# A block-diagonal product of 576 columns as two products of 288 columns in a two-bank PSUM tile

## The chip, the cores and the metric

One core of one Trainium2 chip runs the whole program. The metric is the device time of one execution in microseconds. Engine names in the profile: PE is TensorE, PEld its weight loads, DVE is VectorE, ACT is ScalarE, POOL is GpSimd, SP is SyncE.

## The reference, cut to what matters

```python
kv  = einsum('bhsd,bhse->bhde', k, v)          # 8 x 8 heads, 576 tokens, 64 wide
out = einsum('bhsd,bhde->bhse', q, kv)
x   = out / sqrt(mean(out * out) + 1e-6) * g_norm
h   = x.reshape(4608, 512) @ w_in              # 512 -> 2048
y   = (h * erf(softplus(h))) @ w_out           # 2048 -> 512
```

Nearly all the work is in the last two products. The attention part is small, and the kernel slips it between them, pair of heads by pair of heads.

## The kernel before

The tokens go in groups. A group of the large products has 512 tokens: the first 512 of each of the eight sequences, and a ninth group made of the 64 left over from each ("tail"). While PE works on one group, the attention of the next is computed for its four pairs of heads. From the third group on, the mean of squares is taken from a high and a low part in the faster fp32r format (on the chain of before 0.23 us for 512 columns, against 0.86 for the two records of an fp32 product, L520); the code calls that `halves`. (The prediction and the code count groups from 0, so the changed groups are 2 to 7; the expectations of the runs count from 1 and say 3 to 8.)

The kernel keeps eight PSUM buffers of [128, 512] fp32, here called banks. Six serve the large products. Two, the pool `ps_at`, serve the attention, with four one-bank tiles per pair that take turns:

```python
def bank(name):                                 # one bank: [128, 512] fp32
    pool, tag = (pools or {}).get(name, (ps_at, "at"))
    return pool.tile([P, G], FP32, name=name, tag=tag)

def products():
    kv_ps = st["kv"] = bank("kv_ps")
    ...                                         # PE: k.T v of two heads into kv_ps
    if p % 2 == 0:                              # PE: tail of q, transposed, for two pairs
        nc.tensor.transpose(kv_ps[:, q_tail], q_last[:, p // 2], ident)
    ...
    for i in range(2):                          # DVE: the two blocks to SBUF
        nc.vector.tensor_copy(out=bd[s, s], in_=kv_ps[s, s])
    if p % 2 == 0:
        tails[T] = attp.tile([P, P], FP32, name="qT_last", tag="t")
        nc.vector.tensor_copy(out=tails[T], in_=kv_ps[:, q_tail])
    st["tail"] = tails[T][:, p % 2 * R : p % 2 * R + R]
    qt_ps = bank("qt_ps")
    for j in range(J):                          # PE: q transposed
        nc.tensor.transpose(qt_ps[:, j * P : j * P + P], qs[:, j], ident)
    nc.scalar.copy(st["qT"], qt_ps)             # ACT

def apply():
    qT, o_ps, kv_ps = st["qT"], bank("se_ps"), st.pop("kv")
    nc.tensor.matmul(kv_ps[:, o_tail], lhsT=bd, rhs=st.pop("tail"), ...)   # 64 columns
    nc.tensor.matmul(o_ps, lhsT=bd, rhs=qT, ...)                           # 512 columns
    nc.vector.tensor_copy(out=x_last[...], in_=kv_ps[:, o_tail])
    nc.scalar.activation(qT, o_ps, AF.Square)
# then halve() [DVE], mean() [PE, ACT], norm() [DVE: u, u, x], split() [ACT, DVE]
```

The pieces stand at fixed places among the large products: `products` at the head of a batch, `apply` two products later, and so on. In the timelines of this case the engines work through their instructions in the order in which the code issues them: in before a kv is done at 658.3 us, but VectorE, with the last eviction (e) ahead of that copy, stands idle for 0.46 us until that can run at 660.98, and copies kv at 661.59.

## Time and profile before

| | before |
|---|---|
| time, median of the first three runs | 954.99 us (953.88 to 955.01) |
| span of the profiled run | 952.2 us |
| PE busy | 929.1 us, 98% |
| mean granted clock of PE | 0.998 |
| pair to pair in the steady part, kv to kv | 24.72 and 24.84 us in turn |

PE is the bound. The lines of the page, of the chain of waits and of PE's timeline that carry this are in the prediction below.

### The profile page before, as it was taken

Reading aid. Unit: us, or ns where it says so; the run is one execution under the profiler, and the core shown is the slowest. Engines: PE = TensorE matmul, PEld = TensorE weight load, DVE = VectorE, ACT = ScalarE, POOL = GpSimd, SP = SyncE. Lnnn points to the kernel's source line nnn. Section 1 sums busy time; section 2 is a strip of 40 time slices with the busy share of each in tenths; the row PEclk is TensorE's granted clock in tenths of the full one; section 3 lists DMA queues with packets and bytes.
Section 4 is the critical chain, followed back from the end, with each engine's and each line's share of the span. In section 5 each row is a group of like instructions: output and inputs, shape, how many; then the busy total and the mean of one; then the engine's idle time right before and its main releaser. Section 6 shows DMA issues by size and latency. Waiting matters only on the chain.

```text
span 952.2 us, 11746 instructions
## 1 busy us (share of the span) xinstructions
PE 929.1 (98%) x4272; PEld 684.7 (72%) x4272; DVE 740.4 (78%) x1054; ACT 616.1 (65%) x825; POOL 2.4 (0%) x10
## 2 busy tenths in 40 slices
PE   6999999999998999999999999999999999999998
PEld 4444445665686788888888888888888788878886
DVE  3979958888575888888888888887887877777667
ACT  3889876777665666666666666666666666665552
POOL 1000000000000000000000000000000000000000
PEclk9999999999999999999999999999999999999999
DMA  9856505899699888898899988988896779768872
GB/s 256 276 163 212 167 9 218 307 347 337 212 356 339 275 286 282 289 315 301 290 304 309 303 293 314 322 290 283 290 337 251 264 256 348 283 248 304 338 272 65
DMA packets 111842, 259.78 MB, mean 273 GB/s; under 512 B 43864, under 2 KB 69544, under 8 KB 111784
## 3 DMA queue, kind: packets, MB, share of 16 engines
q1 hardware_dynamic: 110152, 256.73, 78.1%
q10 hardware_dynamic: 1568, 2.29, 0.8%
q8 instruction: 34, 0.56, 0.2%
q14 instruction: 24, 0.20, 0.1%
q0 software_dynamic: 64, 0.00, 0.0%
HBM read 224.40 MB, written 34.60 MB: 272 GB/s over the span
## 4 chain that ended last, share of the span: by engine, by line
PE 83%; ACT 6%; DVE 6%; DMA 3%; SPq 1%; issue 1%; DVEq 0%; ACTq 0%
PE n_ps L462 42%; PE m_ps L462 21%; PE o_ps L520 8%; PE h_ps L691 3%; PE se_ps L325 3%; PE kv_ps L297 2%; PE qt_ps L319 2%; DMA out_dram<-e 1%; DMA w_in_parts<-w_in 1%; SPq L136 1%; ACT w_e L215 1%; ACT L103 1%; DVE h L445 1%; ACT w_m L219 1%; DMA q_sb<-in_q_dram 1%
## 5 line engine op out<-in xcount | busy, mean ns | idle before, releaser
L462 PE MATMUL n_ps<-x_forms,w_in_parts 128*128 128x512 f32 x896 | 234.9, 404 | 5.0 <-ACT h L834 3.4
L462 PE MATMUL n_ps<-w_out_parts,g_forms 128*128 128x512 f32 x928 | 231.3, 391 | 0.0
L462 PEld LDWEIGHTS n_ps<-x_forms,w_in_parts 128*128 128x128 f32 x896 | 167.6, 189 | 49.4 <-issue 9.3
L462 PEld LDWEIGHTS n_ps<-w_out_parts,g_forms 128*128 128x128 f32 x928 | 174.2, 188 | 38.4 <-issue 1.7
L836 ACT ACTIVATE s<-h 128x512 f32<-128x512 f32 x112 | 71.1, 635 | 180.5 <-DVE h L445 180.5
L445 DVE TENSOR_TENSOR h<-m_ps,h 128x512 f32<-128x512 f32 x116 | 79.8, 688 | 68.3 <-ACT h L834 48.9
L462 PE MATMUL m_ps<-w_out_parts,g_forms 128*128 128x512 f32 x464 | 124.2, 389 | 0.0
L462 PE MATMUL m_ps<-x_forms,w_in_parts 128*128 128x512 f32 x448 | 120.0, 390 | 0.0
L520 PE MATMUL o_ps<-w_out_sb,h_sb 128*128 128x512 f32 x224 | 100.8, 593 | 0.3 <-DVE h_sb L642 0.3
L462 PEld LDWEIGHTS m_ps<-w_out_parts,g_forms 128*128 128x128 f32 x464 | 87.1, 188 | 18.1
L462 PEld LDWEIGHTS m_ps<-x_forms,w_in_parts 128*128 128x128 f32 x448 | 84.3, 188 | 17.8
L445 DVE TENSOR_TENSOR e<-m_ps,e 128x512 f32<-128x512 f32 x116 | 80.2, 692 | 17.9 <-PE m_ps L462 10.5
L440 DVE SCALAR_TENSOR_TENSOR e<-n_ps,e 128x512 f32<-128x512 f32 x88 | 60.3, 685 | 37.6 <-PE n_ps L462 37.5
L520 PEld LDWEIGHTS o_ps<-w_out_sb,h_sb 128*128 128x128 f32 x224 | 42.3, 190 | 48.9 <-issue 46.6
L834 ACT ACTIVATE h<-n_ps 128x512 f32<-128x512 f32 x112 | 65.6, 586 | 13.4 <-DMA out_dram<-e 9.5
L411 DVE SCALAR_TENSOR_TENSOR g_forms<-g_forms 128x1024 fp32r<-128x1024 f32 x58 | 71.1, 1225 | 2.0
L408 DVE TENSOR_TENSOR g_forms<-h,g_forms 128x1024 fp32r<-128x1024 f32 x58 | 70.6, 1217 | 1.8 <-ACT g_forms L405 1.4
L405 ACT ACTIVATE g_forms<-h 128x1024 fp32r<-128x1024 f32 x58 | 58.9, 1060 | 12.4 <-PE m_ps L462 9.8
L854 DVE TENSOR_TENSOR h<-h,s 128x1024 f32<-128x1024 f32 x56 | 65.9, 1218 | 0.7 <-ACT s L840 0.7
L691 PE MATMUL h_ps<-xT,w_in_sb 128*128 128x512 f32 x144 | 64.9, 594 | 0.8 <-DVE w_in_sb L240 0.6
L106 ACT ACT_TABLE_LOAD x44 | 56.5, 1283 | 0.7
L840 ACT ACTIVATE s<-s 128x1024 f32<-128x1024 f32 x56 | 56.2, 1052 | 0.3
(98 smaller groups left out, 1014.9 us busy)
## 6 DMA issues: line engine op xcount, KB each, us to landing
w_out_parts<-w_out SPq DMA_DIRECT2D x116, 768.0 KB
w_in_parts<-w_in SPq DMA_DIRECT2D x112, 768.0 KB
w_in<-w_new SPq DMA_DIRECT2D x16, 768.0 KB
q_sb<-in_q_dram SPq DMA_DIRECT2D x32, 256.0 KB
w_raw<-in_moe_w_out_dram SPq DMA_DIRECT2D x8, 1024.0 KB
out_dram<-e SPq DMA_DIRECT2D x32, 256.0 KB
k_sb<-in_k_dram SPq DMA_DIRECT2D x28, 287.5 KB
v_sb<-in_v_dram SPq DMA_DIRECT2D x28, 287.5 KB
```

Of the source, the lines that this page charges most:

```text
L106: nc.scalar.preload_act_table_set("softplus")
L405: nc.scalar.activation(high, x, AF.Copy, scale=1.0 + 2.0**-13)
L408: nc.vector.tensor_tensor(out=low, in0=x, in1=high.bitcast(FP32), op=ALU.subtract)
L411: nc.vector.scalar_tensor_tensor(out=both, in0=low.bitcast(FP32), scalar=SHIFT, in1=high.bitcast(FP32), op0=ALU.mult, op1=ALU.add,)
L440: nc.vector.scalar_tensor_tensor(out=out_, in0=ps, scalar=scale, in1=out_, op0=ALU.mult, op1=ALU.add)
L445: nc.vector.tensor_tensor(out=out_, in0=ps, in1=out_, op=ALU.add)
L462: nc.tensor.matmul(ps, lhsT=weights(form, k), rhs=moving(form, k), start=(form == forms[0] and k == 0), stop=(form == forms[-1] and k == 3),)
L520: nc.tensor.matmul(o_ps[j], lhsT=g[:, j * P : j * P + P], rhs=w_out_sb[:, f, :], start=(f == 0), stop=last,)
L691: nc.tensor.matmul(plain[i], lhsT=w_in_sb[:, c, i % FC * P : i % FC * P + P], rhs=xT[T][:, c, :], start=(c == 0), stop=(c == KC - 1),)
L834: nc.scalar.activation(h[:, i], n_ps, AF.Copy, scale=SHIFT - 1.0)
L836: nc.scalar.activation(s[:, i], h[:, i], AF.Softplus)
L854: nc.vector.tensor_tensor(out=part(h, half), in0=part(h, half), in1=part(s, half), op=ALU.mult)
```

## The change

The intent: two products of 288 columns carry the same 576 tokens in less time. In before the two products take 1.08 us, where 576 columns at the 0.858 us of 512 (two records of 0.429) would take 0.97. My estimate put the 0.11 us between these two numbers down to weight loads that the 64-column product is too short to cover. For this the tile has two banks, with 256 columns of the product and 32 of the tail in each, and the means go beside them in the other 256 columns. The diff, cut to its core:

```diff
         def bank(name):
+            if T >= FIRST:
+                return two_banks()[:, name in ("qt_ps", "se_ps")]
+        def two_banks():
+            if "two" not in st:
+                st["two"] = ps_two.tile([P, 2, G], FP32, name="at_ps", tag="at")
+            return st["two"]
 ...
-            if p % 2 == 0:
-                tails[T] = attp.tile([P, P], FP32, name="qT_last", tag="t")
-                nc.vector.tensor_copy(out=tails[T], in_=kv_ps[:, q_tail])
+            if halves:
+                tail = tails.pop(T) if p % 2 else kv_ps[:, P : P + R]
+                nc.vector.tensor_copy(out=st["qT"][:, :, HG:], in_=twofold(tail))
+                if p % 2 == 0:
+                    tails[T] = attp.tile([P, R], FP32, name="qT_next", tag="t")
+                    nc.vector.tensor_copy(out=tails[T], in_=kv_ps[:, P + R : 2 * P])
 ...
         def apply():
+            if halves:
+                for i in range(2):
+                    nc.tensor.matmul(two[:, i, : HG + HR], lhsT=bd, rhs=qT[:, i], ...)
+                nc.vector.tensor_copy(out=..., in_=two[:, :, HG : HG + HR])
+                nc.scalar.activation(qT, two[:, :, :HG], AF.Square)
 ...
         def mean(table=True):
+                for i in range(2):
+                    nc.tensor.matmul(ms[:, i], lhsT=mean_w, rhs=hi[:, i], start=True, stop=False)
+                    nc.tensor.matmul(ms[:, i], lhsT=mean_w, rhs=lo[:, i], start=False, stop=True)
 ...
+            at_room.close()
+            ps_two = ctx.enter_context(tc.tile_pool(name="ps_two", bufs=1, space=PSUM))
```

## The prediction

> **What bounds the kernel now.** I read the page first: the busy line, then the chain of work that ended last.
>
> ```profile
> PE 929.1 (98%) x4272; PEld 684.7 (72%) x4272; DVE 740.4 (78%) x1054; ACT 616.1 (65%) x825; POOL 2.4 (0%) x10
> ...
> PE 83%; ACT 6%; DVE 6%; DMA 3%; SPq 1%; issue 1%; DVEq 0%; ACTq 0%
> PE n_ps L462 42%; PE m_ps L462 21%; PE o_ps L520 8%; PE h_ps L691 3%; PE se_ps L325 3%; PE kv_ps L297 2%; PE qt_ps L319 2%; DMA out_dram<-e 1%; DMA w_in_parts<-w_in 1%; SPq L136 1%; ACT w_e L215 1%; ACT L103 1%; DVE h L445 1%; ACT w_m L219 1%; DMA q_sb<-in_q_dram 1%
> ```
>
> TensorE (PE) is the bound; the rest matters only where it makes PE stand. A busy matmul engine need not be at its peak, so I read the chain of waits in order of time, over one pair of heads in the steady part (columns: start us, us on the chain, what):
>
> ```profile
> 607.97 0.73 PE kv_ps L297 x20
> 608.71 0.26 PE kv_ps L305
> 608.97 0.44 PE qt_ps L319 x4
> 609.40 1.85 PE n_ps L462 x8
> ...
> 614.89 0.17 PE kv_ps L324 x2
> 615.06 0.91 PE se_ps L325 x2
> 615.98 1.84 PE n_ps L462 x8
> ...
> 624.17 0.23 PE ms_ps L346
> 624.40 0.23 PE ms_ps L347
> 624.63 1.83 PE n_ps L462 x8
> ```
>
> The chain here is PE without a hole, so an instruction that PE saves is time saved, and one that it gains is time lost. The diff touches three of these lines: L324 (tail product, 64 columns), L325 (block-diagonal product, 512 columns) and L346/L347 (mean of squares, high and low parts). "x2" for one matmul of the code says that an fp32 matmul runs as two passes; the fp32r mean runs as one.
>
> From 255 us to the end PE does stand in places, which I found in the timeline of PE (bracket: idle time, what ended it):
>
> ```profile
> 293.86 3.68 PE L462 MATMUL n_ps<-x_forms,w_in_parts 128*128 128x512 f32 x8 [3.41 <-ACT h L834]
> ...
> 309.87 0.80 PE L297 MATMUL kv_ps<-v_sb,k_sb 116*64 116x64 f32 x20
> 310.60 0.33 PE L305 MATMUL kv_ps<-ident,q_last 128*128 128x128 f32 x1
> 311.39 0.66 PE L319 MATMUL qt_ps<-ident,q_sb 128*128 128x128 f32 x4 [0.45 <-DVE x L378]
> ```
>
> The first is an h tile that waits for the store of e (the page puts 9.5 us of ACT's idle time before L834 on that DMA). The second matters to the change: kv of the next pair starts while the previous pair is still being normalised, and only the transposes wait for x, the last reader of the previous pair's product.
>
> [...] four 128-column transposes take 0.44 us on the chain, 0.11 each, although each weight-load record is about 190 ns long. [...] The trace has 227 in fp32r (0.91 for four m_ps) and 429 per fp32 pass (o_ps: 3.43 us for eight), so an fp32 pass streams at about half that rate. [...]
>
> **The change part by part**, per pair; groups 2 to 7 have 6 x 4 = 24 pairs.
>
> (1) Product, before: 0.17 + 0.91 = 1.08 us. Two 512-column passes at 0.429 are 0.86; the tail's two passes therefore cost 0.22, that is 0.11 each. [...] After: two matmuls of 288 columns, four passes. 0.429 x 288/512 = 0.241, say 0.243; four give 0.97. [...] Gain 0.11 us. The columns are the same (576)[...].
>
> (2) Mean: two fp32r matmuls of 512 columns, 0.46 us, become four of 256. [...] Four give 0.48. Loss 0.02.
>
> (3) DVE: twelve 128x128 tail copies of 292 ns go (L315), -3.5 us; 24 PSUM copies of 128x64 at 216 ns (as L326) come, +5.2, and 12 SBUF ones. For those: 128x512 casts take 418 ns and 128x1024 shifts 689 (L338, L207), so 0.53 ns a column and 147 fixed: 181 ns, +2.2 us. Sum +3.9 us on an engine with 22% idle. They stand behind the bd_kv copies, at 612.1 in the pair above; the product starts at 614.7. The new copies end by 612.6: hidden.
>
> (4) Buffers. Kv and transposes used to take whichever of two one-bank buffers was free; now one two-bank tile is reused, so kv, too, must wait for x. In the steady part:
>
> ```profile
> 631.74 0.75 DVE L378 SCALAR_TENSOR_TENSOR x<-se_ps,gm_col,u 128x512 f32<-128x512 f32 x1
> ...
> 632.74 0.80 PE L297 MATMUL kv_ps<-v_sb,k_sb 116*64 116x64 f32 x20
> ```
>
> x ends at 632.49; a handover takes 0.04 to 0.05 us (311.34 to 311.39). Slack is 0.2 us: no stall, but little. In the second to fourth pairs after the store's stall (309.87, 335.38, 360.10) kv starts before x has ended: 1.47, 0.52 and 0.30 us before. At 309.87 kv and the tail transpose, 0.73 + 0.2, now run after 311.38 instead of in the shadow of x; PE stood for 0.45 to 0.8 there anyway, so the transposes come about 0.75 us later. That delay also lets DVE and ACT catch up, so the next two (0.52, 0.30) should cost nothing more. Loss 0.75 us, once.
>
> Sum: 24 x (0.11 - 0.02) = 2.2 us gained. The four pairs of group 2 (0.36) lie ahead of the stall at 293, which ends with a DMA, and are probably swallowed there. 20 x 0.09 = 1.8; less 0.75 leaves about 1.05 us: 954.99 - 1.05 = 953.9.
>
> **Rivals.** (a) *Kv's wait for x becomes a stall in every pair.* For: slack is only 0.2 us, and u, x and the three ACT steps before them now read and write two runs of 256. Against: DVE's cost on cut patterns shows no extra per run: L854 works on four runs of 256 in 1218 ns[...]. If the chain grew by 0.3 us, 20 pairs would lose 0.1 to 0.2 each: 956 to 957. (b) *Weight loads become visible.* If a 256-column fp32r matmul were held to the 190 ns of a load record, the mean would cost 0.76, +0.3 a pair, +5 us net: 959 to 960. The transposes at 0.11 speak against. (c) *The tail comes free*: removing it saves all 0.22 a pair, 5 us, 950. Against: its 64 columns still stream. (d) *ACT's Square waits for DVE's copy of the tail.* In the steady part DVE copies at 618.33 to 618.54 and Square starts at 618.98, already in that order; in group 2 Square would come up to 1 us later (copy 153.18, Square 152.36), with ACT idle 3.7 us after it. Worth under 0.5 us in all.
>
> **Range and chances.** The certain terms are tenths of a microsecond a pair; 2% of 955 is 19 us, or 0.8 us on each of 24 pairs. Nothing above makes that: even (b) is a quarter of it. Three runs of before spread by 1.1 us, and the stretch held by DMA may move by a microsecond or two either way. So 951.0 to 957.0, faster 0.005, same 0.985, slower 0.01.
>
> **What would show it right or wrong.** Product lines on the chain at 0.97 us instead of 1.08; mean at 0.48 instead of 0.46; no PE idle before kv in the steady part; at the second pair of group 3 an idle time before kv, ended by x, of about 1.5 us, and none before the transposes; DVE busy up by about 4 us; n_ps and m_ps untouched. It is wrong if kv waits in every pair, if a mean matmul takes more than 0.13 us, if four product passes take more than 1.05 us, or if the stall at 293 changes by more than 2 us.

## More of the kernel before

From the timeline of before (start us, length us, engine, line, operation, out<-in, shapes, count):

```profile
657.46 0.80 PE L297 MATMUL kv_ps<-v_sb,k_sb 116*64 116x64 f32 x20
...
658.36 0.60 PE L319 MATMUL qt_ps<-ident,q_sb 128*128 128x128 f32 x4
...
661.59 0.45 DVE L312 COPY bd_kv<-kv_ps 64x64 f32<-64x64 f32 x2
```

kv is in PSUM at 658.3, and the transposes of q follow at once, but VectorE copies kv only at 661.6. In its order of work the copies stand behind the last evictions of the batch (e) and the splitting of x (x_forms). Before the change nobody waits for that copy until `apply`, some 6 us after kv.

## The result and the profile after

Median 1061.80 us over four runs (1059.78 to 1065.17), against 954.49 us for before in the same rounds. A ratio here is the mean time of one kernel's fast runs over that of the other's of the same rounds, so it is not quite the ratio of the medians. It is 1.113, interval 1.110 to 1.116. The outputs are right.

The page of the changed kernel, its busy line and the granted clock in 40 slices (tenths):

```profile
PE 970.5 (91%) x4320; PEld 722.4 (68%) x4320; DVE 746.0 (70%) x1078; ACT 624.0 (59%) x825; POOL 2.4 (0%) x10
...
PEclk9999999999998888899888889999888899999999
```

PE is busy 41.4 us longer than before (970.5 - 929.1), and idle 69.8 us longer: 1063.4 - 970.5 = 92.9 against 952.2 - 929.1 = 23.1. The two sum to the growth of the span, 111.2 us. The clock, which was full in every slice of before, falls in the part where attention runs.

What ended PE's idle times, from the list of its waits (total us, times, longest):

```profile
PE at_ps L345 <- DVE bd_kv L331: 38.0, 12, 3.5
PE at_ps L345 <- DVE qT_next L337: 36.2, 12, 3.6
```

L345 is the transposes of q. They wait 24 times, once per pair, for VectorE's last read of kv: in the second and fourth pairs that is the copy to bd_kv, in the first and third the copy to qT_next. In before, this wait does not exist. The chain of waits in order of time shows one of them (start us, us, what):

```profile
658.80 0.61 DVE x_forms L455
659.41 0.02 issue
659.43 0.69 DVE x_forms L458
660.12 0.13 DVE bd_kv L331
660.25 0.01 issue
660.26 0.24 DVE bd_kv L331
660.50 0.04 issue
660.55 0.66 PE at_ps L345 x4
...
666.67 0.97 PE at_ps L356 x4
```

VectorE is no later than in before: from the start of kv to bd_kv it takes 3.8 us here (656.27 to 660.04) and 4.1 us there. But PE now stands until VectorE has come through the evictions, x_forms and bd_kv. The timeline of PE puts that stall at 3.48 us. The last line is the new product: 0.97 us.

The lower clock follows the stalls. Busy time of each engine in four stretches of the changed kernel (columns: stretch, its length, PE, PEld, DVE, ACT, POOL, then the granted clock, DMA share and GB/s):

```profile
344.80:351.60 6.80, 4.92 (x39) 3.81 (x37) 6.52 (x10) 2.80 (x4) 0.00 (x0) 1.00 0.94 357
351.60:358.40 6.80, 5.21 (x15) 4.25 (x16) 4.12 (x7) 3.09 (x4) 0.00 (x0) 0.50 0.13 51
358.40:382.30 23.90, 22.24 (x116) 18.02 (x114) 16.18 (x24) 13.27 (x17) 0.00 (x0) 1.00 0.85 287
382.30:389.10 6.80, 4.88 (x14) 4.00 (x15) 3.85 (x8) 2.80 (x4) 0.00 (x0) 0.50 0.11 43
```

PE idles from 349.7 to 353.2; at 351.6 its clock drops to half for 6.83 us; then it is full for 23.9 us, until the next stall halves it again. The trace's record of the clock has 20 such spells, each of 3.41 or 6.83 us (the last is cut by the end), 119.9 us in all; before had two, 4.9 us. In each trace all begin on one grid of 3.413 us, and the full-speed stretches between them are whole multiples of it, too (23.893 us is 7, 112.640 is 33); I call one step of that grid a window. PE need not have been idle for a whole window: the drop at 351.6 comes 1.9 us into the stall, after a window (348.2 to 351.6) in which PE was busy up to 349.7. Experiment 8 says how much idle time it took. So the matmuls behind a stall take longer, and rows of untouched products look dearer. The first product of a batch, before and after:

```profile
L462 PE MATMUL n_ps<-x_forms,w_in_parts 128*128 128x512 f32 x896 | 234.9, 404 | 5.0 <-ACT h L834 3.4 <-DVE x_forms L408 0.7 <-ACT x_forms L405 0.7
```

```profile
L509 PE MATMUL n_ps<-x_forms,w_in_parts 128*128 128x512 f32 x896 | 258.4, 435 | 1.5 <-DVE x_forms L455 0.7 <-ACT x_forms L452 0.7
```

These 896 matmuls, busy 23.5 us longer, are the same instructions; they stand right behind the transposes.

### The profile page after: what moved, and what is told of

Same layout as the page of the kernel before. It is cut to its first block, busy times and chain, and to the rows that moved or that the text cites. A ratio compares the mean times of both kernels' runs of the same rounds, so it can differ in the third digit from the quotient of the medians.

```text
span 1063.4 us, 11956 instructions
## 1 busy us (share of the span) xinstructions
PE 970.5 (91%) x4320; PEld 722.4 (68%) x4320; DVE 746.0 (70%) x1078; ACT 624.0 (59%) x825; POOL 2.4 (0%) x10
## 4 chain that ended last, share of the span: by engine, by line
PE 55%; DVE 18%; issue 1%; ACT 1%; DVEq 0%
PE n_ps L509 34%; PE m_ps L509 16%; DVE h L903 4%; DVE e L492 4%; PE at_ps L345 2%; PE at_ps L356 2%; DVE e L487 2%; DVE x L425 1%; DVE u L416 1%; DVE x_forms L458 1%; DVE x_forms L455 1%; DVE u L413 1%; DVE bd_kv L331 1%; DVE e L824 1%; PE at_ps L394 0%
## 5 line engine op out<-in xcount | busy, mean ns | idle before, releaser
L509 PE MATMUL n_ps<-x_forms,w_in_parts 128*128 128x512 f32 x896 | 258.4, 435 | 1.5 <-DVE x_forms L455 0.7
L509 PEld LDWEIGHTS n_ps<-x_forms,w_in_parts 128*128 128x128 f32 x896 | 185.4, 210 | 43.9 <-DVE x_forms L455 1.6
L509 PE MATMUL m_ps<-x_forms,w_in_parts 128*128 128x512 f32 x448 | 127.3, 408 | 0.0
L509 PEld LDWEIGHTS m_ps<-x_forms,w_in_parts 128*128 128x128 f32 x448 | 91.7, 205 | 21.5
L345 PE MATMUL at_ps<-ident,q_sb 128*128 128x128 f32 x96 | 23.2, 386 | 74.2 <-DVE bd_kv L331 38.0
L347 ACT COPY qT<-at_ps 128x512 f32<-128x512 f32 x24 | 14.1, 587 | 107.6 <-PE at_ps L345 107.6
L345 PEld LDWEIGHTS at_ps<-ident,q_sb 128*128 128x128 f32 x96 | 14.8, 191 | 78.1 <-DVE bd_kv L331 39.7
```

Source lines behind the costliest of these rows:

```text
L509: nc.tensor.matmul(ps, lhsT=weights(form, k), rhs=moving(form, k), start=(form == forms[0] and k == 0), stop=(form == forms[-1] and k == 3),)
```

## The experiments

The theory after the result: the waits are placed by tile, not by bank. kv (bank 0) and the transposes (bank 1) lie in one tile, so a write to the one waits for all earlier reads of the other by another engine. The rivals: the new shapes or the reads across two banks are dear in themselves; or kv's new wait for x is the stall.

### 1. Transposes first

```diff
+            if halves:                     # ahead of VectorE's copies
+                qt_ps = bank("qt_ps")
+                for j in range(J):
+                    nc.tensor.transpose(qt_ps[:, j * P : j * P + P], qs[:, j], ident)
             for i in range(2): ...         # bd_kv and tail copies, as before
-            qt_ps = bank("qt_ps")          # (kept for groups without halves)
```

> The changed kernel with one edit: in groups 3 to 8 the four transposes of q are issued before the copies of bd_kv and of the tail, so nothing that VectorE does stands before them in program order. Theory (the transposes wait for VectorE's reads of kv only because both lie in one tile, though in different banks): no idle time of PE before the transposes, granted clock back at 0.998, and what the prediction had summed for the rest, 953.9 us, say 952.5 to 955.5. Rival A (products of 288 and 256 columns, or reads across two banks, are dear in themselves): it stays above 1000 us. Rival B (kv's new wait for x is the stall): idle time appears before kv instead, 1 to 3 us in each pair, 980 to 1030 us.

Measured: 980.46 us median (979.57 to 981.21), ratio to before 1.028, interval 1.027 to 1.029; clock 0.998. The wait before the transposes and the low clock are gone, and with them 81 us of 107. Rival A falls, since the shapes and the two-bank reads are still there. But 26 us stay, and they are what rival B named: PE idles before kv, 1.4 to 1.6 us in each pair.

```profile
PE at_ps L316 <- issue: 27.0, 18, 1.6
```

The list names no releaser for these waits, but the timeline does fit x: in the pair below, x ends at 651.41 and kv starts at 651.51.

Why is x late here, when in before it ended 0.2 us in time? The timeline of this run around one pair:

```profile
652.25 0.66 PE L331 MATMUL at_ps<-ident,q_sb 128*128 128x128 f32 x4
...
655.44 0.45 DVE L335 COPY bd_kv<-at_ps 64x64 f32<-64x64 f32 x2
...
655.98 0.59 ACT L352 COPY qT<-at_ps 128x512 f32<-128x512 f32 x1 [3.90 <-DVE bd_kv L335]
```

The transposes are done at 652.9, but ScalarE copies them to qT only at 655.98, after VectorE's copies of kv. Both only read, and in different banks; still one waits for the other, because it is one tile and VectorE's copies come first in the code. The two also write to one SBUF tile, qT, in different columns; that is not the wait, for VectorE's copy to qT runs from 655.92 to 656.12, while ScalarE is already writing. ScalarE stands idle for 3.9 us, and all that it does afterwards is later, down to the Ln, Exp and Square of the norm. That is a new form of the theory, to be tested: a second wait of the same kind.

### 2. Old shapes, one tile

The kernel before with nothing but the shared tile:

```diff
         def bank(name):
+            if T >= FIRST:
+                if "two" not in st:
+                    st["two"] = ps_two.tile([P, 2, G], FP32, name="at_ps", tag="at")
+                return st["two"][:, int(name in ("qt_ps", "se_ps"))]
```

> The kernel before with one part of the change alone: from the third group on the four one-bank tiles of a pair are the two halves of one two-bank tile; the products keep their old shapes (64 and 512 columns, mean in 512). Theory (shared tile): the whole loss is here too, 1055 to 1068 us, 3.5 us of idle PE before the transposes of nearly every pair, clock about 0.95. Rival A (the new shapes cost it): 954 to 957 us, no idle.

Measured: 1061.52 us (one run), clock 0.955. Waits of PE:

```profile
PE at_ps L324 <- DVE bd_kv L317: 38.1, 12, 3.5
PE at_ps L324 <- DVE qT_last L320: 35.4, 12, 3.5
```

The same loss without one changed product. The tile alone is enough.

### 3. Filling the wait

```diff
+            if halves and T > FIRST:
+                fill = pool.tile([P, G], FP32, name="fill", tag=tag)   # the next product's bank
+                for _ in range(12):
+                    nc.tensor.matmul(fill, lhsT=mean_w, rhs=x_forms[T - 1][0][:, 0], ...)
             qt_ps = bank("qt_ps")
```

> The changed kernel with twelve useless fp32r matmuls of 512 columns (12 x 0.227 = 2.7 us) ahead of the transposes of groups 4 to 8, into the bank that the next product overwrites; VectorE's work and the wait stay. Theory (the loss has two terms: about 74 us of idle PE, and about 31 us because PE's clock is halved for a while after a stall of 3.5 us without matmuls): PE idles 0.6 to 0.9 us before the transposes instead of 3.5, the clock is 0.99 or more in that stretch, and the time falls by about the clock's term, to 1028 to 1036 us. Rival (the lower clock has another cause than PE's idling, or the term is small): clock stays near 0.95 and the time at 1058 to 1066.

Measured: 1026.55 us (one run), a little below the expected range. One pair, and the stretch from 340 to 700 us:

```profile
663.45 0.66 PE L352 MATMUL at_ps<-ident,q_sb 128*128 128x128 f32 x4 [0.77 <-DVE qT_next L337]
```

```profile
340.00:700.00 360.00, 352.04 (x1787) 284.55 (x1786) 258.16 (x376) 201.84 (x265) 0.00 (x0) 1.00 0.78 262
```

The wait ends when it ended before, yet useless work made the kernel 35.25 us faster (1061.80 - 1026.55), because PE's clock stays full (0.998 for the run, against 0.945 in the changed kernel). So of the 107.3 us between the medians about 35 are clock and about 72 are waiting. That the clock drops because PE idles, and not for another cause, is shown by this run.

### 4. The first edit for every other pair

```diff
-            if halves:                     # experiment 1
+            if halves and p % 2:
                 qt_ps = bank("qt_ps")
                 for j in range(J):
                     nc.tensor.transpose(...)
```

> The edit of the first run for the second and fourth pair of each group only; 12 of the 24 pairs keep the wait. Theory: half the loss, 1000 to 1015 us; PE idles about 3.5 us before the transposes of even pairs only. If the clock's loss needed stalls close to each other, less: 990 to 1000. If one order of issue were to upset the other pairs, more than 1020.

Measured: 1023.11 us (one run), clock 0.975. This is above what I gave for plain halves, and falls in the third case that I had named, that one order of issue upsets the other pairs. The edited pairs lose the stall but delay ScalarE, as in experiment 1, so the pair that follows begins with 1.26 to 1.61 us of idle time before kv and then has its own stall of 3.74 us. The run says that pairs are not independent; it was sent together with experiment 1, before that second wait was known.

### 5. The copy first, too

```diff
             if halves:                     # ahead of VectorE's copies
                 qt_ps = bank("qt_ps")
                 for j in range(J):
                     nc.tensor.transpose(qt_ps[:, j * P : j * P + P], qs[:, j], ident)
+                nc.scalar.copy(st["qT"][:, :, :HG], twofold(qt_ps))
```

> The changed kernel with the transposes of q and ScalarE's copy of them to qT issued ahead of VectorE's copies. Theory (in the first run what was left, 1.5 us of idle PE before kv in each pair, is a second wait of the same kind: ScalarE's copy of bank 1 waits for VectorE's copies of bank 0, ScalarE falls 3 us behind, so u, x and with them kv come late): ScalarE's copy starts within 0.1 us of the transposes' end, idle PE before kv under 0.1 us in the steady part, 952.5 to 955.5 us. Rival (kv's wait for x is dear by itself, since the two-bank tile comes free only at x): idle before kv of 0.5 us or more stays in each pair, 965 to 981 us.

Measured: 954.47 us median over six runs (951.63 to 955.65), ratio to before 0.9999, interval 0.998 to 1.001. ScalarE's copy follows the transposes at once (their end is 634.62), and in the steady part PE never waits:

```profile
633.97 0.65 PE L332 MATMUL at_ps<-ident,q_sb 128*128 128x128 f32 x4
...
634.66 0.59 ACT L333 COPY qT<-at_ps 128x512 f32<-128x512 f32 x1 [1.02 <-PE at_ps L332]
```

```profile
340.00:700.00 360.00, 360.00 (x1864) 295.70 (x1863) 292.14 (x430) 230.19 (x306) 0.00 (x0) 1.00 0.89 299
```

The new theory held and the rival fell: kv's wait for x costs nothing in the steady part when ScalarE is in time. Two places in the order of issue, within the one tile, were the whole loss.

### 6. The copy first, with the old shapes

Experiment 2's kernel in the order of experiment 5:

```diff
+            if halves:
+                qt_ps = bank("qt_ps")
+                for j in range(J):
+                    nc.tensor.transpose(qt_ps[:, j * P : j * P + P], qs[:, j], ident)
+                nc.scalar.copy(st["qT"], qt_ps)
             for i in range(2): ...         # VectorE's copies out of kv
```

> The kernel before, with the shared two-bank tile and the order of the run above, but the old shapes (64 and 512 columns, mean in 512). If the new shapes gain what the prediction summed (0.09 us a pair, 20 to 24 pairs), this is 1.8 to 2.2 us above the run above: 955 to 957 us; product lines 1.08 us on PE's chain against 0.97, mean 0.46 against 0.48. If shapes don't matter, both are equal within 0.5 us. If the order is not the cure with these shapes, 975 or more.

Measured: 953.39 us median (953.25 to 955.88), ratio to before 0.9992, interval 0.998 to 1.001. By whole times, old and new shapes can't be told apart; the expected 1.8 to 2.2 us are not seen. The traces do tell them apart, in the steady part. Starts of kv, pair to pair, in us:

```
before                  24.72  24.84  in turn
copy first, old shapes  24.72  24.84  in turn
copy first, new shapes  24.65  24.77  in turn
```

The new shapes gain 0.07 us a pair, some 1.4 us over 20 pairs. The profiled run of experiment 5 gave more than that back at one place: its stall at 290 us was 3.97 us against 1.61 in this run, with 6.8 us of half clock behind it against none. (Shorter waits near 300 and 311 us differ as well, the other way, by 0.8 to 0.9 us each.) What makes that stall vary between runs is not settled.

### 7. A slightly shorter wait

The transposes between VectorE's two copies to bd_kv:

```diff
             for i in range(2):
                 s = slice(i * D, i * D + D)
                 nc.vector.tensor_copy(out=bd[s, s], in_=kv_ps[s, s])
+                if halves and i == 0:
+                    qt_ps = bank("qt_ps")
+                    for j in range(J):
+                        nc.tensor.transpose(...)
```

> The changed kernel with the transposes issued between VectorE's two copies of bd_kv: the wait ends 0.2 us (odd pairs) to 0.6 us (even pairs) earlier, so PE idles about 3.2 and 3.0 us instead of 3.5 and 3.6; that is under the 3.41 us that the low-clock spells come in. If the clock's loss starts only at a stall of about that length, the clock is 0.99 and the time near 1020 to 1032 us; if it grows with any stall, the clock stays near 0.95 to 0.96 and the time at 1045 to 1058.

Measured: 1065.12 us (one run), clock 0.942. The waits did shrink as expected:

```profile
595.24 1.11 PE L335 MATMUL at_ps<-ident,q_sb 128*128 128x128 f32 x4 [3.23 <-DVE bd_kv L331]
```

PE's idle time summed from the trace fell from 82.4 us in the changed kernel to 72.9 (gaps over 0.02 us between matmuls), the half-clock time rose from 119.9 to 126.3, and the time did not fall at all. It is above both ranges that I gave. By the clock of the whole run (0.942, against 0.945 in the changed kernel) the stalls of 3.0 to 3.2 us here halved it no less than those of 3.5 did there. From the second pair of group 4 on (counted from 0), pairs follow each other at 30.68 to 30.73 us; nine windows of 3.413 us are 30.72. The changed kernel comes near it, too: its pairs are 30.6 and 30.8 us apart in turn over most of that stretch. A reading of that: the half-speed spell begins and ends on window edges (all its edges in these traces lie on one grid of 3.413 us), so an earlier end of the wait lies inside a spell that goes on regardless.

### 8. A wait shorter by 0.9 us

Experiment 3 with fewer useless matmuls:

```diff
-                for _ in range(12):
+                for _ in range(4):
```

> The changed kernel with four useless matmuls (0.9 us) ahead of the transposes of groups 4 to 8, so that PE idles about 2.6 us in each of 20 pairs and not 3.5. After the run with the transposes between the copies I hold that the low clock comes in windows of 3.41 us that run on by themselves, and that a pair's period locks to nine of them (30.72 us) because whatever a stall saves in idle time it gives back in half-speed time. Locked: pairs again 30.6 to 30.8 us apart in most of the stretch, 1055 to 1066 us although PE idles 18 us less. Not locked, idle and clock being independent costs: 29.8 us a pair or less, 1040 to 1048 us. If 2.6 us no longer halves the clock, about 1030.

Measured: 1040.99 us (one run), clock 0.982, in the range that I gave for "not locked". But for the first pair, PE idles 2.34 and 2.64 us in turn, and 11 half-speed spells of one window (3.41 us) follow the 20 stalls of these groups. Pairs are 28.2 to 30.2 us apart. So nothing is locked at this length, and the locking of experiment 7 is a reading of the runs with stalls over 3 us only, argued and not shown. At 2.3 to 2.6 us the clock dropped after about every second stall; the count below goes by where a stall falls in a window.

The kept traces give a measure for that. Cut each of the twelve traces, from 12 us on to shortly before its end, into windows of 3.413 us on the grid of its own clock record, and add up PE's idle time in each. Of the windows at full speed, none of the 3215 with up to 1.62 us of idle time was followed by half speed; all 58 with 1.97 us or more were; of the 33 between, 23 were. After a window at half speed, half speed went on in all 49 cases with 0.75 us or more of idle time, and ended in all 81 with 0.49 us or less. So in these traces it is not the length of a stall alone that counts, but how the window edges cut it. By length, the stalls of 3.47 to 3.59 us in the changed kernel were followed by half speed 18 times of 19 (the one at 657.1 us was not), and those of 1.4 to 1.6 us never in the 18 pairs of experiment 1. The stalls of experiment 7 put 2.0 us or more into one window and in most pairs 0.9 to 1.1 us into the next, and so cost two half-speed windows each. In the first 12 us of the traces windows with more idle time than this kept the full clock (in before PE has no matmul until 5.94 us, at full clock); why is not known.

### 9. Two tiles of one bank

The changed kernel in its own order of issue, but with two one-bank tiles. Every instruction that read both banks becomes two.

```diff
-                st["two"] = ps_two.tile([P, 2, G], FP32, name="at_ps", tag="at")
+                st["two"] = [ps_two.tile([P, G], FP32, name=f"at_ps{i}", tag=f"at{i}") for i in range(2)]
 ...
-                nc.scalar.activation(qT, o_ps, AF.Square)
+                for i in range(2):
+                    nc.scalar.activation(qT[:, i], two[i][:, :HG], AF.Square)
```

(and so for the tail copy, Ln, u and x)

> The changed kernel in its own order of issue, with two one-bank tiles in place of the one two-bank tile; each instruction that read both banks becomes two (tail copy, Square, Ln, u, x). Theory (the waits go by tile): no wait of the transposes for VectorE, clock 0.998, and only the dearer norm chain is left, which ends x 0.5 to 1 us later: 956 to 972 us. Rival (the waits come from the order of issue or the new shapes whatever the tiles): above 1040 us.

Measured: 959.32 us (one run), clock 1.000. Order and banks are those of the changed kernel; only the tile is cut, and the waits before the transposes are gone. That separates "by tile" from "by bank" and from "by order alone". What is left is the longer norm: kv begins 0.2 to 0.3 us late in most pairs, and pairs are 25.0 us apart. One such place on the chain, with the transposes (L345) right behind kv and its tail:

```profile
610.01 0.92 PE m_ps L519 x4
610.93 0.28 issue
611.21 0.80 PE at_ps L316 x20
612.01 0.26 PE at_ps L324
612.27 0.44 PE at_ps L345 x4
```

### 10. A version that beats both

The traces of before and of experiment 5 both have one stall of 3.4 to 4.0 us near 290, which ends with the store of the second group's result. The store is issued by SyncE, behind weight loads. On top of experiment 5:

```diff
-            nc.sync.dma_start(out=rows[:, j, :], in_=e)
+            side = nc.gpsimd if T == FIRST - 1 else nc.sync
+            side.dma_start(out=rows[:, j, :], in_=e)
```

> The repaired kernel (transposes and their copy first) with the four stores of the second group's result issued by GpSimd in place of SyncE, so that they don't queue behind weight loads; PE's one stall of 3.4 to 4.0 us near 290 us waits for them. If the store comes earlier: the stall shrinks to under 1 us and its low-clock spell goes, 948.5 to 951 us. If these transfers are held by bandwidth and not by their place in the queue: 952.5 to 955.5, no change.

Measured: 950.96 us median (950.23 to 951.17), before 954.12 in the same rounds; ratio 0.9965, interval 0.9952 to 0.9979. It beats both kernels; against before the gain is only 0.35%, but the interval leaves out 1. The four stores now land 7.0 us after issue (median; KB each, us):

```profile
out_dram<-e POOLq DMA_DIRECT2D x4, 256.0 KB, 7.0
```

In before the store that PE's stall hung on took 9.85 us on the chain, from 283.21 to 293.06. Here the same store is issued no earlier, at 283.25, but lands after 7.09 us. Whether it is the place behind the weight loads that was dear, or another property of SyncE's path, this run does not separate. No idle time at that place is over 0.2 us now, and the clock's record has no half-speed spell before the end. A part is given back 16 us later, where kv waits 1.6 us for x; in experiment 5 that wait was 0.85.

## Why the prediction was wrong, point by point

**Part 1, the product, was right.** 0.97 us was foretold, and the chain after has `PE at_ps L356 x4` at 0.97. That what is saved is weight loads was my estimate; the traces give the times alone. **Part 2, the mean, was right**: 0.48 was foretold, an estimate, and in experiment 5 the chain has four entries of 0.12. Together they give 0.07 us a pair where 0.09 was summed; the 20 pairs that count are worth 1.4 us instead of 1.8. (The "two passes" of an fp32 matmul are two records of the trace, 64 for the 32 products of L325 in before. Each takes 429 ns at 512 columns, against 227 for the one record of an fp32r matmul; the sum rests on the measured time, not on the count of passes.)

**Part 3 failed in its last word, "hidden".** VectorE's busy time grew by 5.6 us (740.4 to 746.0; 3.9 foretold), which is harmless. But I asked only whether the copies end before the product, 2 us later. I didn't ask whether anything else that is issued behind them touches the same tile. The transposes do. In before they start at 658.36 us, and VectorE comes to kv at 661.59.

**Part 4 is the step that failed**: it put the cost of the shared tile at one wait of kv for x, 0.75 us in all, where the runs show 24 waits of the transposes for VectorE's reads of kv, 74.2 us, and the half clock after them. It says: "now one two-bank tile is reused, so kv, too, must wait for x." It took one tile for a question of when the tile comes free to the next pair. Inside one pair I went on thinking in banks, while the waits of the program go by tile in these runs: a write waited for the earlier reads of the tile by another engine (24 waits of the transposes, 73.5 us, in experiment 2; none in experiment 9, with two tiles), and a read waited for an earlier read by another engine as well (ScalarE's copy to qT, 3.90 us idle in experiment 1; in experiment 5 it starts 0.04 us after the transposes). What the program's own waits go by, I did not ask. The range of 951 to 957 had no room for it, and no rival named it. Rival (a), kv stalled by x in every pair, did come up in experiment 1, but as a consequence of ScalarE's being late. The two runs of 256 cost VectorE nothing extra: u takes 684 ns and x 751 in both kernels (L366 and L378 before, L413 and L425 after; medians).

**The consequences that no step had.** A wait of 3.5 us in each pair also costs clock, about 35 us of the 107 (experiment 3). The wait before kv at the second pair of group 3 does exist, but its size was not hit: about 1.5 us of idle time was foretold, at a net cost of 0.75; the traces have 0.85 us in experiment 5, 1.62 in experiment 10 and 1.73 in experiment 6, against 0.45 us before the transposes in before. The working for 0.75 was loose as well: kv and the tail's transpose, 0.93 us, move behind x whole, so 0.9 follows from its own numbers.

**Once the two orders of issue are changed, the time lies in the foretold range**: 953.9 foretold, 954.47 measured for experiment 5. But before took 954.36 in the same rounds, so the gain is too small to be told from nothing, and the agreement does not confirm the sum of 1.05 us.

## What to carry to other kernels

When buffers are merged into one tile, list for every engine what it does to that tile in the order of issue, and ask of each neighbouring pair on different engines whether it needs the wait that it now gets; issue first what others are waiting for. A repeated stall of PE can cost clock as well, here about 35 us on top of 72 us of waiting; after the first 12 us it did in these traces wherever 1.97 us or more of idle time fell into one window of 3.413 us, so price such a stall above its length. And where only a read's place in the code makes it late, moving a line is a cheaper cure than undoing the layout.
